# Sparse attention and two feed-forward layers in one kernel: moving the first block's feed-forward pieces among the attention units

## The chip, the cores and the metric

The kernel runs on one core of a Trainium2 chip (one of its eight NeuronCores). The metric is the device time of one execution in microseconds (us), the median over several runs. A profile of one execution comes with it; its span is the time from the first to the last profiled instruction.

## The reference

```
x = attention(q, k, v)          # 2 batches, 8 heads, 768 tokens, 64 per head; ALiBi bias, local window of 96 and 8 global keys
x = x.reshape(1536, 512)
h = x @ w_in                    # 512 x 2048
x = (h * sigmoid(h)) @ w_out    # 2048 x 512
h = x @ w_in2
out = (h * clip(h + 3, 0, 6) / 6) @ w_out2
```

The weights come as float64 and the result is float32. A float32 operand of a feed-forward product is split into a high and a low part, so that each product is three matmuls (high by high, high by low, low by high).

## The kernel before, in words

Everything is in one function. The program of each engine is written by a loop over steps n (`loop`, line 782), which emits the attention work of step n, then at most one piece of feed-forward work, then the transposes of the unit before, then late work of ScalarE (ACT) and the decoding of weights. TensorE (PE), ACT and GpSimd (POOL) run their instructions in just that order; the order on VectorE (DVE) is found by a list scheduler.

**Attention** is cut into 16 units of three steps (unit u is steps 3u to 3u+2): a batch, half of its 768 tokens and a pair of heads. A unit's chain is: transposes of q and k (`stage_a`, psA, copied out by ACT as kt at L330 and qt at L327), scores (psS, L363), bias and row minimum on DVE (L375, one instruction for each of six tiles), exponentials on ACT (L379, six instructions, two in each step), normalising on POOL (L389), transposes of the result (psT, L399, in the next unit, copied out by DVE as pt_0 and pt_2 and by ACT as pt_1), values (psO, L417, one unit later still), copied out as xh (ACT, L420) and xl (DVE, L421).

**The feed-forward** goes through the hidden dimension in eight chunks of 256 for each layer. A chunk's work on a block of tokens is two h pieces (`h_piece`, 12 matmuls, psH) and four y pieces (`y_piece`, 6 matmuls, psY). An h piece is followed by `gate_tile`: tanh on ACT (a, L505), the product on DVE (g, L512, it reads the same PSUM bank), the high part on ACT (gh, L518) and the low part on POOL (gl, L525). A y piece of the first chunk is copied out by ACT (L681). For the first chunk the blocks are 384 tokens long, and the blocks' outputs xh, xl become complete unit by unit, so most of this chunk stands among the attention units.

The list `stream` (lines 706 to 735) holds the pieces, and `when(i)` gives the step of piece i: every second step from step 17 (the last step of unit 5) on, and every step from 53 on. In the first block `None` stands for the y pieces that there are none of. In these steps all h and y pieces share one PSUM bank, the only one with the tag "f":

```
ps_bufs = {"S": 2, "o": 2, "tr": 3, "f": 1}
ring = ({"h": ("f",), "y": ("f",)}, ...)[ready[0]][kind]
```

While the units run, the weights of the next chunk are decoded beside them: da and dc on ACT (L103, L107), three instructions on DVE of which the first two are L1013 and L1019, sums on POOL, high parts on ACT (L145).

Of the kernel before, what the change touches and what calls it, by code (L numbers as in the profile page):

```python
# [28 lines left out]
def attention_ffn_kernel(ctx, tc, q, k, v, n_global, n_local, w_in1, w_out1, w_in2, w_out2, out):  # L29
    nc = tc.nc  # L30
# [9 lines left out]
    FC = 2  # L40
# [3 lines left out]
    KT = DM // P  # L44
# [17 lines left out]
    def bank(tag, name):  # L62
        return psum.tile([P, 512], F32, name=name, tag=tag, bufs=ps_bufs[tag])

    xh = xpool.tile([P, KT, NTOK], F32R, name="xh", tag="xh")
    xl = xpool.tile([P, KT, NTOK], F32R, name="xl", tag="xl")
# [88 lines left out]
    def fast(l, c):  # L155

        return c > 1
# [40 lines left out]
    PRE = 3 * NP + LAG + 1  # L198
# [3 lines left out]
    def blocks(l, c):  # L202
        return [(t, t + TB) for t in range(0, NTOK, TB)] if (l, c) == (0, 0) else BLOCKS


    beside = 3 * 6

    def when(i):
        return PRE + 2 * i if i < beside else PRE + beside + i

    slots = {}

# [253 lines left out]
    def ffn_bank(kind, name):  # L466
        ring = ({"h": ("f",), "y": ("f",)}, {"h": ("f", "S", "S"), "y": ("tr", "o", "tr", "o", "tr")}, {"h": ("S",), "y": ("f", "o", "o")})[ready[0]][kind]
        tag = ring[rot[kind] % len(ring)]
        rot[kind] += 1
        return bank(tag, name)  # L470

    def h_piece(l, c, tk, j):
        w = weights[l, c]
        ih, il = w["ih"], w["il"]
        n0, n1 = tk
        ps = ffn_bank("h", f"psH{l}_{c}_{n0}_{j}")[:, :n1 - n0]
        js = slice(j * P, (j + 1) * P)
        n = 0
        for kt in range(KT):
            for a, x in ((ih, xh), (ih, xl), (il, xh)):  # L480
                nc.tensor.matmul(ps, a[:, kt, js], x[:, kt, n0:n1], start=n == 0, stop=n == 3 * KT - 1)  # L481
                n += 1
        gate_tile(l, c, tk, j, ps)

    def gate_tile(l, c, tk, j, ps, wait=0):

        n0, n1 = tk
        if (l, c, n0) not in gs:
            if fast(l, c) and n0 == FB:
                g1 = late_pool.tile([P, 2, FC, FB], F32R, name=f"g1{l}_{c}", tag="g1")  # L490
                gs[l, c, n0] = [g1[:, 0], g1[:, 1]]
            else:
                gs[l, c, n0] = [fpool.tile([P, FC, n1 - n0], F32R, name=f"g{x}{l}_{c}_{n0}", tag=f"g{x}") for x in "hl"]
        gh, gl = gs[l, c, n0]
        t = {}
        silu = l == 0 and ready[0] > 0
        name = f"{l}_{c}_{n0}_{j}"

        def act():

            t["a"] = fpool.tile([P, n1 - n0], F32, name=f"a{name}", tag="a")
            if silu:
                nc.scalar.activation(out=t["a"], in_=ps, func=AF.Silu)
            elif l == 0:
                nc.scalar.activation(out=t["a"], in_=ps, func=AF.Tanh, scale=0.5)  # L505
            else:
                nc.scalar.activation(out=t["a"], in_=ps, func=AF.Relu, bias=three)

        def gate():
            op = dict(scalar=1.0, op0=ALU.add) if l == 0 else dict(scalar=6.0, op0=ALU.min)  # L510
            t["g"] = fpool.tile([P, n1 - n0], F32, name=f"g{name}", tag="g")
            nc.vector.scalar_tensor_tensor(out=t["g"], in0=t["a"], in1=ps, op1=ALU.mult, **op)  # L512

        def hi():
            if silu:
                nc.scalar.mul(gh[:, j, :], t["a"], 2.0)
            else:
                nc.scalar.copy(gh[:, j, :], t["g"])  # L518

        def lo():  # L520
            if silu:
                nc.vector.scalar_tensor_tensor(out=gl[:, j, :], in0=t["a"], scalar=2.0, in1=gh[:, j, :].bitcast(F32),
                                               op0=ALU.mult, op1=ALU.subtract)
            else:
                (nc.vector if ready[0] else nc.gpsimd).tensor_tensor(out=gl[:, j, :], in0=t["g"], in1=gh[:, j, :].bitcast(F32), op=ALU.subtract)  # L525

        if wait:
            late.setdefault(now[0] + wait, []).append(act)
        else:
            act()  # L530
        if not silu:
            rests.setdefault(now[0] + wait + 1, []).append(gate)
        late.setdefault(now[0] + wait + 1, []).append(hi)
        rests.setdefault(now[0] + wait + 2, []).append(lo)
# [171 lines left out]
    stream, first_piece = [], {}  # L706
    Y = lambda l, c, b: [(y_piece, l, c, BLOCKS[b], m) for m in range(KT)]
    H = lambda l, c, b: [(h_piece, l, c, BLOCKS[b], j) for j in range(FC)]
    before = []
    for l, c in chunks:  # L710
        first_piece[l, c] = len(stream)
        if fast(l, c):
            p = [(product, l, c, i) for i in (1, 6, 5, 7, 2, 4, 3)]
            y, before = before, []
            cuts = [0, 2, 3, 4, 5, 6, 7, 8] if len(y) == 8 else [0, 2, 2, 3, 3, 4, 4, 4]
            for i in range(7):
                stream += [p[i]] + y[cuts[i]:cuts[i + 1]]
            h, y = H(l, c, 2), Y(l, c, 0)
            stream += [h[0]] + y[:2] + [h[1]] + y[2:] if fast(l, c - 1) or not l else h + y
            before = Y(l, c, 1) + Y(l, c, 2)  # L720
            continue
        if (l, c) == (1, 0):

            h = H(l, c, 0) + H(l, c, 1) + H(l, c, 2)
            stream += before[:6]
            first_piece[l, c] = len(stream)
            stream += [h[0]] + before[6:] + h[1:4] + Y(l, c, 0) + h[4:5] + Y(l, c, 1)[:2] + h[5:] + Y(l, c, 1)[2:]
            before = Y(l, c, 2)
            continue
        for tk in blocks(l, c):  # L730
            hs = [(h_piece, l, c, tk, j) for j in range(FC)]
            ys, before = (before or [None] * 4)[:4], before[4:]
            stream += [hs[0], *ys[:2], hs[1], *ys[2:]]
            before += [(y_piece, l, c, tk, m) for m in range(KT)]
    stream += before

# [9 lines left out]
    for n, (i, j) in enumerate(pieces):  # L746
        ahead = aheads(i)[j]
        for off, f in decode(n):
            slots.setdefault(when(first_piece[chunks[i]]) - ahead + off, []).append(f)
        if j == 1 and fast(*chunks[i]):  # L750
            for off, f in sums(i):
                slots.setdefault(when(first_piece[chunks[i]]) - 4 + off, []).append(f)

    with tc.manual_schedule(engines=None):
# [23 lines left out]
        stage_a(0, 1)  # L778
        warm_up(1, P)
    todo = {when(i): f for i, f in enumerate(stream)}  # L780

    def loop(n):
# [280 lines left out]
```

## Time and profile before

| what | value |
|---|---|
| median of three runs | 614.27 us (613.48 to 614.62) |
| the profiled execution's own time | 613.77 us |
| its span | 611.9 us |
| PE busy | 597.8 us, 98% |
| DVE, ACT, POOL busy | 476.6, 418.2, 155.1 us |
| granted TensorE clock | 1.00 throughout |

The end of a matmul is modelled, and matmuls overlap, so PE's busy share is high even where it waits; what a piece takes is read from the start of its first matmul to the start of the next piece. The attention units end at about 120 us, and from about 127 us on PE runs feed-forward pieces without a gap.

### The profile page before, as it was taken

To read this page: it belongs to the slowest core of one execution; us is meant where nothing else is said; L and a number is where in the kernel's file an instruction comes from. 1 tells how busy PE (TensorE), PEld (TensorE's weight loads), DVE (VectorE), ACT (ScalarE), POOL (GpSimd) and SP (SyncE) were. 2 spreads that over 40 slices of the span, in tenths; PEclk is the share of its full clock that TensorE was granted. 3 is DMA by queue.
4 is the path that set the end of the run, shared out by engine and by line. 5 is a ranking of instruction groups with operands and counts; after the bars stand their busy time and mean duration, and the time that the engine had idled before them with its cause. 6 is when DMAs were issued, how large, how long until landed. Compare 5 with 4: busy or idle time off the path is not lost.

```text
span 611.9 us, 9407 instructions
## 1 busy us (share of the span) xinstructions
PE 597.8 (98%) x3144; PEld 493.9 (81%) x3144; DVE 476.6 (78%) x1049; ACT 418.2 (68%) x868; POOL 155.1 (25%) x233
## 2 busy tenths in 40 slices
PE   8899999999999999999999999999999999999996
PEld 5677788898888888888888888888888888888885
DVE  6887888886876868686766789978979797979453
ACT  5988988666666666575756767766767676757660
POOL 3777676801111111111111210011111111121200
PEclk9999999999999999999999999999999999999999
DMA  7866653205758677777777772477496868776544
GB/s 191 192 161 149 150 142 98 61 1 120 159 135 185 159 176 169 172 171 172 174 162 146 171 175 69 153 187 180 101 217 161 189 156 179 166 174 137 104 114 166
DMA packets 76426, 92.43 MB, mean 151 GB/s; under 512 B 52180, under 2 KB 52436, under 8 KB 76116
## 3 DMA queue, kind: packets, MB, share of 16 engines
q0 software_dynamic: 11520, 43.00, 37.2%
q1 hardware_dynamic: 64304, 48.54, 26.9%
q8 instruction: 27, 0.44, 0.3%
q10 hardware_dynamic: 548, 0.23, 0.1%
q14 instruction: 27, 0.22, 0.1%
HBM read 45.61 MB, written 3.15 MB: 80 GB/s over the span
## 4 chain that ended last, share of the span: by engine, by line
PE 93%; ACT 2%; DVE 2%; POOL 1%; issue 1%; DMA 0%; SPq 0%; POOLq 0%; ACTq 0%
PE psY L667 42%; PE psH L481 21%; PE psP_b L562 8%; PE psP_c L562 5%; PE psP_a L562 5%; PE psO L417 3%; PE psS_S L363 2%; PE psT L399 2%; PE psA L325 2%; PE psS_o L363 1%; PE psW L426 1%; ACT z L379 1%; DVE pt L404 1%; POOL z L389 0%; DVE z L375 0%
## 5 line engine op out<-in xcount | busy, mean ns | idle before, releaser
L696 POOL DMA_DIRECT2D y<-st x78 | 68.0, 872 | 361.6 <-ACT st L692 357.0
L692 ACT COPY st<-psY 128x512 f32<-128x512 f32 x156 | 91.2, 585 | 53.0 <-PE psY L667 49.3
L481 PE MATMUL psH<-xh,wih 128*128 128x512 f32 (+1 forms) x200 | 76.7, 383 | 0.5 <-ACT y L681 0.5
L481 PE MATMUL psH<-xl,wih 128*128 128x512 f32 (+1 forms) x200 | 76.4, 382 | 0.0
L481 PE MATMUL psH<-xh,wil 128*128 128x512 f32 (+1 forms) x200 | 76.3, 381 | 0.0
L667 PE MATMUL psY<-gh,woh 128*128 128x512 f32 (+1 forms) x152 | 58.3, 384 | 0.5 <-DVE mn L375 0.5
L667 PE MATMUL psY<-gh,wol 128*128 128x512 f32 (+1 forms) x152 | 57.5, 378 | 0.0
L667 PE MATMUL psY<-gl,woh 128*128 128x512 f32 (+1 forms) x152 | 57.4, 378 | 0.0
L667 PE MATMUL psY<-wol,gh 128*128 128x512 f32 x142 | 55.2, 389 | 0.0
L667 PE MATMUL psY<-woh,gh 128*128 128x512 f32 x142 | 55.2, 389 | 0.0
L667 PE MATMUL psY<-woh,gl 128*128 128x512 f32 x142 | 55.2, 389 | 0.0
L379 ACT ACTIVATE z<-z,mn 128x256 f32<-128x256 f32 (+1 forms) x96 | 46.3, 486 | 9.1 <-DVE mn L375 8.6
L103 ACT ACTIVATE da<-raw 128x512 f32<-128x512 f32 x64 | 43.1, 673 | 11.8 <-DMA raw<-in_moe_w_in_dram 7.7
L389 POOL TENSOR_SCALAR z<-z,sm 128x256 f32<-128x256 f32 (+1 forms) x96 | 43.5, 471 | 23.4 <-DVE sm L385 16.5
L1025 DVE SCALAR_TENSOR_TENSOR da<-raw,da 128x512 int32<-128x512 int32 x64 | 45.7, 714 | 1.0
L579 DVE TENSOR_TENSOR u<-psP_c,u 128x512 f32<-128x512 f32 x24 | 16.5, 687 | 37.7 <-ACT u L573 37.7
L481 PEld LDWEIGHTS psH<-xh,wih 128*128 128x128 f32 x200 | 37.6, 188 | 7.7 <-ACT y L681 1.2
L481 PEld LDWEIGHTS psH<-xl,wih 128*128 128x128 f32 x200 | 37.5, 188 | 7.0 <-DVE xl L591 0.4
L481 PEld LDWEIGHTS psH<-xh,wil 128*128 128x128 f32 x200 | 37.5, 188 | 6.9 <-POOL wil L148 0.4
L1013 DVE TENSOR_SCALAR da<-da 128x512 f32<-128x512 f32 x64 | 28.6, 446 | 14.3 <-ACT da L103 14.3
L129 DVE SCALAR_TENSOR_TENSOR dc<-raw,de 128x512 f32<-128x512 uint32 x56 | 38.5, 687 | 1.5 <-DVE de L1030 0.8
L134 DVE TENSOR_TENSOR dc<-dc,da 128x512 f32<-128x512 f32 x56 | 38.3, 684 | 0.4
(196 smaller groups left out, 1498.3 us busy)
## 6 DMA issues: line engine op xcount, KB each, us to landing
y<-st POOLq DMA_DIRECT2D x78, 512.0 KB, 4.9
raw<-in_moe_w_in_dram SPq DMA_DIRECT2D x32, 512.0 KB, 4.2
raw<-in_moe_w_out_dram SPq DMA_DIRECT2D x32, 512.0 KB, 3.4
rk<-in_k_dram SPq DMA_DIRECT2D x32, 96.0 KB, 3.2
rv<-in_v_dram SPq DMA_DIRECT2D x32, 96.0 KB, 2.2
rq<-in_q_dram SPq DMA_DIRECT2D x31, 96.0 KB, 3.1
out_dram<-y SPq DMA_DIRECT2D x11, 256.0 KB, 2.5
y<-yf POOLq DMA_DIRECT2D x2, 1024.0 KB, 6.6
```

The source lines that it names most:

```text
L103: nc.scalar.activation(out=t["a"], in_=raws[n][:, :, 1].bitcast(F32), func=AF.Abs)
L129: nc.vector.scalar_tensor_tensor(out=t["c"], in0=raws[n][:, :, 0].bitcast(U32), scalar=2.0 ** -52, in1=t["e"].bitcast(F32), op0=ALU.mult, ...
L134: engine.tensor_tensor(out=t["c"], in0=t["c"], in1=t["a"], op=ALU.add)
L379: nc.scalar.activation(out=z[:, t, h, :w], in_=z[:, t, h, :w], func=AF.Exp, bias=mn[:, t, h:h + 1], scale=-1.0, accum_out=sums_of[u][:, t, ...
L389: nc.gpsimd.tensor_scalar(out=z[:, t, h, :w], in0=z[:, t, h, :w], scalar1=smt[u][:, t, h:h + 1], scalar2=1.0, op0=ALU.mult, op1=ALU.mult)
L481: nc.tensor.matmul(ps, a[:, kt, js], x[:, kt, n0:n1], start=n == 0, stop=n == 3 * KT - 1)
L562: nc.tensor.matmul(ps, a[:, 2 * k + q, f * P:(f + 1) * P], x, start=p in (1, 5) and n == 0, stop=n == 5, skip_group_check=True)
L667: nc.tensor.matmul(ps[:, :rhs.shape[1]], lhs, rhs, start=n == 0, stop=n == 3 * FC - 1)
L692: nc.scalar.copy(st[:, m % 2, :], part)
L696: late.setdefault(n, []).append(lambda: nc.gpsimd.dma_start(y, st, accum_op=ALU.add))
L1013: nc.vector.tensor_scalar(out=a, in0=a, scalar1=as_float(897 << 20), scalar2=as_float((1151 << 20) - 1), op0=ALU.max, op1=ALU.min)
L1025: nc.vector.scalar_tensor_tensor(out=ai, in0=w1, scalar=-0x40000000, in1=ai, op0=ALU.bitwise_and, op1=ALU.bitwise_or)
```

## The change

The first block has two h pieces (j = 0 and 1); each is now emitted in two halves of six matmuls (the first two and the last two of the four 128-row slices of d_model), which accumulate in one bank. The four halves stand in the last steps of units 5, 6, 7 and 8 (steps 17, 20, 23, 26). The `None` entries are gone. From unit 9 on an h piece stands in the last step of every odd unit (29, 35, 41, 47, as before), and the two y pieces that follow it in the second and third step of the even unit between (31, 32, 37, 38, 43, 44, 49, 50); before, the first stood in the second step of the even unit and the second in the first step of the odd one (31, 33, 37, 39 and so on). From step 53 on the steps are the same.

```
+    STEPS = [PRE + 3 * i for i in range(4)] + [PRE + 12 + 6 * i + j for i in range(4) for j in (0, 2, 3)]
+
     def when(i):
-        return PRE + 2 * i if i < beside else PRE + beside + i
+        return STEPS[i] if i < len(STEPS) else PRE + beside + beside - len(STEPS) + i
...
-    def h_piece(l, c, tk, j):
+    begun = {}
+
+    def h_piece(l, c, tk, j, halves="ab"):
...
-        ps = ffn_bank("h", f"psH{l}_{c}_{n0}_{j}")[:, :n1 - n0]
+        if "a" in halves:
+            begun[0] = ffn_bank("h", f"psH{l}_{c}_{n0}_{j}")[:, :n1 - n0]
+        ps = begun[0]
...
+            if "ab"[kt * 2 // KT] in halves:
...
+        if "b" in halves:
+            gate_tile(l, c, tk, j, ps)
...
-            hs = [(h_piece, l, c, tk, j) for j in range(FC)]
-            ys, before = (before or [None] * 4)[:4], before[4:]
-            stream += [hs[0], *ys[:2], hs[1], *ys[2:]]
+            halves = ("a", "b") if not stream else ("ab",)
+            hs = [[(h_piece, l, c, tk, j, half) for half in halves] for j in range(FC)]
+            ys, before = before[:4], before[4:]
+            stream += [*hs[0], *ys[:2], *hs[1], *ys[2:]]
```

What this does to the engines' programs, at three places. The lines of the changed kernel are numbered two higher from line 208 on, six higher in `gate_tile` and `y_piece`, seven higher in the decoding functions.

**PE and ACT, units 10 and 11.** Before, PE's first y piece (psY_0_0_0, y of block 0, rows 0 to 127 of the output) is followed by the transposes psT; the words in brackets are the engines it has to wait for:

```order
L325 MATMUL psA_1_1308<-ident,rq_1084 128x128 x2
L667 MATMUL psY_0_0_0_1319<-gh_0_0_749,woh_885 128x384 [waits DVE_49]
L667 MATMUL psY_0_0_0_1319<-gl_0_0_750,woh_885 128x384
L667 MATMUL psY_0_0_0_1319<-gh_0_0_749,wol_886 128x384 [waits Pool_49]
L399 MATMUL psT_0_1337<-ident,z_1131 128x128 [waits DVE_49,Pool_49]
```

and in the change the second y piece stands between them and waits for ACT:

```order
L327 MATMUL psA_1_1308<-ident,rq_1072 128x128 x2
L673 MATMUL psY_0_0_0_1319<-gh_0_0_856,woh_881 128x384 [waits DVE_49]
L673 MATMUL psY_0_0_0_1319<-gl_0_0_857,woh_881 128x384 [waits Pool_49]
L673 MATMUL psY_0_0_0_1319<-gh_0_0_856,wol_882 128x384
L673 MATMUL psY_0_0_1_1337<-gh_0_0_856,woh_881 128x384 [waits Activation_49]
L401 MATMUL psT_0_1345<-ident,z_1127 128x128 [waits DVE_49]
```

ACT's program there, before (z are exponentials):

```order
L327 ACTIVATE qt_1284<-psA_1_1308,small 128x384
L681 COPY y_0_1326<-psY_0_0_0_1319 128x384
L379 ACTIVATE z_1254,eps_89<-z_1254,mn_1255 128x256 x2
L402 COPY pt_1_1347<-psT_1_1342 128x512
L103 ACTIVATE da_1357<-raw_702 128x512
L379 ACTIVATE z_1369,eps_90<-z_1369,mn_1370 128x128 x2
L420 CAST xh<-psO_1376 128x384
L330 COPY kt_1396<-psA_0_1398 128x3x128
L681 COPY y_0_1326<-psY_0_0_1_1404 128x384
```

and in the change:

```order
L329 ACTIVATE qt_1284<-psA_1_1308,small 128x384
L687 COPY y_0_1326<-psY_0_0_0_1319 128x384
L381 ACTIVATE z_1254,eps_89<-z_1254,mn_1255 128x256 x2
L687 COPY y_0_1326<-psY_0_0_1_1337 128x384
L404 COPY pt_1_1355<-psT_1_1350 128x512
L103 ACTIVATE da_1365<-raw_702 128x512
L381 ACTIVATE z_1377,eps_90<-z_1377,mn_1378 128x128 x2
```

The copy of the second y piece moved from the odd unit to the even one, ahead of pt_1. The same pattern stands in units 12, 13 and 14, 15.

**DVE, at the start of unit 13.** Before, the first score tile of unit 13 (z_1613) comes ahead of the decoding of the next weights (da):

```order
L404 COPY pt_2_1596<-psT_2_1591 128x512
L384 TENSOR_REDUCE sm_1501<-eps_89 128x2
L375 ISA z_1613,mn_1614<-psS_S_1601,distA 128x256
L375 ISA mn_1614 128x1
L385 RECIPROCAL sm_1501<-sm_1501 128x2
L375 ISA z_1613,mn_1614<-psS_S_1602,distA 128x256
L1013 TENSOR_SCALAR da_1599<-da_1599 128x512
```

and in the change two instructions of the decoding stand ahead of the first score tile:

```order
L406 COPY pt_0_1590<-psT_0_1587 128x2x128
L406 COPY pt_2_1604<-psT_2_1599 128x512
L1020 TENSOR_SCALAR da_1607<-da_1607 128x512
L1026 TENSOR_SCALAR da_1607<-da_1607 128x512
L377 ISA z_1621,mn_1622<-psS_S_1609,distA 128x256
```

The scheduler put L1020 and L1026 (L1013 and L1019 before) in front of unit 13's scores; at unit 15 it is the same, at unit 11 only the first of them.

**PE, units 5 and 6.** Before, unit 5 has a whole h piece ahead of its transposes, and unit 6 none; in the change each has half of one. Unit 5 in the change:

```order
L327 MATMUL psA_1_715<-ident,rq_514 128x128 x2
L487 MATMUL psH_0_0_0_736<-xh,wih_444 128x384
L487 MATMUL psH_0_0_0_736<-xl,wih_444 128x384
L487 MATMUL psH_0_0_0_736<-xh,wil_445 128x384
L401 MATMUL psT_0_743<-ident,z_561 128x128 [waits Activation_49,Pool_49]
L401 MATMUL psT_1_750<-ident,z_561 128x128 [waits DVE_49,Pool_49]
L401 MATMUL psT_2_757<-ident,z_561 128x128 [waits Activation_49,Pool_49]
```

The three kinds of psH rows come twice. The last group, psT_2, waits for ACT's qt in units 5 to 8 (in units 6 and 8 before it waited for DVE alone).

## Rows read from the trace of the kernel before

**Rows 1.** The page, part 1: busy us, share, instructions of each engine.

```profile
PE 597.8 (98%) x3144; PEld 493.9 (81%) x3144; DVE 476.6 (78%) x1049; ACT 418.2 (68%) x868; POOL 155.1 (25%) x233
```

**Rows 2.** Windows: busy us (instructions) of PE, PEld, DVE, ACT, POOL; clock; DMA.

```profile
37.35:71.22 33.87, 31.94 (x312) 26.73 (x309) 27.53 (x112) 29.38 (x91) 26.10 (x45) 1.00 0.68 164
71.22:99.76 28.54, 27.72 (x252) 23.67 (x250) 24.04 (x92) 25.38 (x78) 20.35 (x34) 1.00 0.56 138
```

**Rows 3.** Timeline of PE, units 12 and 13: start, duration, group, [idle before <-releaser].

```profile
86.78 0.42 PE L667 MATMUL psY<-gh,woh 128*128 128x384 f32 x1
...
87.92 0.82 PE L399 MATMUL psT<-ident,z 128*128 128x128 f32 x6
...
92.53 0.42 PE L667 MATMUL psY<-gh,woh 128*128 128x384 f32 x1
...
94.40 0.45 PE L481 MATMUL psH<-xh,wih 128*128 128x384 f32 x1 [0.24 <-ACT y L681]
```

**Rows 4.** Timeline of ACT, units 12 to 14.

```profile
85.30 0.51 ACT L379 ACTIVATE z<-z,mn 128x256 f32<-128x256 f32 x1 [0.97 <-DVE mn L375]
...
88.99 0.47 ACT L681 COPY y<-psY 128x384 f32<-128x384 f32 x1
...
90.34 0.57 ACT L402 COPY pt<-psT 128x512 f32<-128x512 f32 x1
90.81 0.71 ACT L103 ACTIVATE da<-raw 128x512 f32<-128x512 f32 x1
91.39 0.53 ACT L379 ACTIVATE z<-z,mn 128x256 f32<-128x256 f32 x1
...
93.87 0.48 ACT L681 COPY y<-psY 128x384 f32<-128x384 f32 x1 [0.57 <-PE psY L667]
...
99.76 0.51 ACT L379 ACTIVATE z<-z,mn 128x256 f32<-128x256 f32 x1 [1.04 <-DVE mn L375]
```

**Rows 5.** Timeline of DVE, units 12 and 13.

```profile
84.84 0.42 DVE L375 CUSTOM_DVE_ANT_0 z<-psS_S,distA 128x256 f32<-128x256 f32 x1
...
91.55 0.76 DVE L1013 TENSOR_SCALAR da<-da 128x512 f32<-128x512 f32 x1
```

**Rows 6.** The page, part 5: the same line over the whole span, busy, mean ns.

```profile
L1013 DVE TENSOR_SCALAR da<-da 128x512 f32<-128x512 f32 x64 | 28.6, 446 | 14.3 <-ACT da L103 14.3
```

**Rows 7.** Timeline of ACT, units 10 and 11.

```profile
71.22 0.40 ACT L379 ACTIVATE z<-z,mn 128x128 f32<-128x128 f32 x1 [1.17 <-DVE mn L375]
...
74.69 0.47 ACT L681 COPY y<-psY 128x384 f32<-128x384 f32 x1
...
77.10 0.39 ACT L379 ACTIVATE z<-z,mn 128x128 f32<-128x128 f32 x1
```

**Rows 8.** Timeline of PE, units 5 and 6.

```profile
42.45 0.50 PE L363 MATMUL psS_S<-kept,qt 64*128 64x128 f32 x4
...
48.15 0.63 PE L399 MATMUL psT<-ident,z 128*128 128x128 f32 x4 [0.44 <-DVE pt L404]
```

**Rows 9.** Timeline of ACT, units 5 and 6.

```profile
37.35 0.51 ACT L379 ACTIVATE z<-z,mn 128x256 f32<-128x256 f32 x1
...
40.08 0.57 ACT L327 ACTIVATE qt<-psA,small 128x384 f32<-128x384 f32 x1
...
44.21 0.51 ACT L379 ACTIVATE z<-z,mn 128x256 f32<-128x256 f32 x1 [1.45 <-DVE mn L375]
```

**Rows 10.** Timeline of ACT, units 14 and 15.

```profile
103.82 0.53 ACT L681 COPY y<-psY 128x128 f32<-128x128 f32 x2
...
106.37 0.51 ACT L379 ACTIVATE z<-z,mn 128x256 f32<-128x256 f32 x1
```

**Rows 11.** Timeline of PE, from unit 15 to the last block's h piece.

```profile
109.44 0.45 PE L667 MATMUL psY<-gh,woh 128*128 128x384 f32 x1 [0.53 <-DVE mn L375]
...
121.47 0.44 PE L481 MATMUL psH<-xh,wih 128*128 128x384 f32 x1
```

**Rows 12.** Timeline of PE, unit 1: transposes after a long wait.

```profile
15.95 1.06 PE L399 MATMUL psT<-ident,z 128*128 128x128 f32 x8 [0.90 <-DVE kt L335]
```

More of the change, by code (lines that the diff above doesn't have):

```diff
@@ L475, in h_piece @@
         n0, n1 = tk
-        ps = ffn_bank("h", f"psH{l}_{c}_{n0}_{j}")[:, :n1 - n0]
+        if "a" in halves:
+            begun[0] = ffn_bank("h", f"psH{l}_{c}_{n0}_{j}")[:, :n1 - n0]
+        ps = begun[0]
         js = slice(j * P, (j + 1) * P)
-        n = 0
         for kt in range(KT):
[L480 to L483, printed above, removed]
+            if "ab"[kt * 2 // KT] in halves:
+                for a, x in ((ih, xh), (ih, xl), (il, xh)):
+                    nc.tensor.matmul(ps, a[:, kt, js], x[:, kt, n0:n1], start=kt == 0 and x is xh and a is ih, stop=kt == KT - 1 and a is il)
+        if "b" in halves:
+            gate_tile(l, c, tk, j, ps)
     def gate_tile(l, c, tk, j, ps, wait=0):
```

## The prediction

> **What bounds the kernel now.** I read the page first. PE is busy 98% of the span [rows 1], and from about 127 us on the pieces follow each other without a gap, so whatever the change wins or loses among the attention units passes to the end unshortened, and nothing behind them is moved. The windows come next: among the units PE is nearly full, but so is ACT, 29.38 of 33.87 us from unit 5 to unit 10 and 25.38 of 28.54 us from there to unit 14 [rows 2]; the granted clock is 1.00 in both. Then the timelines, engine by engine. The reader should see in them a cycle that is closed by ACT: a unit's first exponentials wait for DVE's minimum of the scores (idle 0.97 to 1.45 us before them [rows 4, 7, 9]), and the rest of ACT's unit runs without a pause. I therefore measure a unit from its first exponentials to the next one's: units 10 and 11 take 85.30 - 71.22 = 14.08 us [rows 4, 7], units 12 and 13 take 99.76 - 85.30 = 14.46 us [rows 4].
>
> **The halves, units 5 to 8.** No matmul is added. A half is six of an h piece's twelve, as many as a y piece has, which takes 1.14 us with its launch (86.78 to 87.92 [rows 3]). Unit 5 loses six; its third group of transposes (four, 0.12 us each) now waits for qt, which ends at 40.08 + 0.57 = 40.65 [rows 9], so unit 6's scores start at about 41.2 in place of 42.45 [rows 8]. ACT idled 1.45 us before unit 6's first exponentials [rows 9], so that they can follow: about 1.2 us won. Unit 6 takes six matmuls; what was a transposing group at 48.15 [rows 8] now waits for qt of unit 7 as well, and its ACT work was already without a pause; I give back 0.3. Unit 7 loses six like unit 5, but behind a unit that is late already: half of what unit 5 gave, 0.6 won. Units 8 and 9 take a half and a gh (0.5 us of ACT) from a neighbour that loses it: nothing. Sum -1.5 us. The bounds: 0, if ACT's idle time only moves, and -4.5, if all of it (33.87 - 29.38 [rows 2]) went; I stay near the first, because qt now stands ahead of the transposes in all four units.
>
> **The y pieces, units 10 to 15.** This is the larger term. Both pieces of an even unit write the one bank "f", and on PE nothing stands between them any more, so the second waits for ACT's copy of the first. ACT does that copy behind the second pair of exponentials and qt: in unit 12 the piece starts at 86.78 and PE is through with it at 87.92 [rows 3], but the copy runs from 88.99 to 89.46 [rows 4]. Before, PE used these 1.5 us for the transposes of the unit before. Now they queue behind the second piece, and behind them the next unit's scores.
>
> One pair worked out, units 12 and 13, counted from unit 12's first exponentials at 85.30. The first copy ends at +4.16, as before, since nothing new stands ahead of it. The second piece runs from +4.2 to +5.3 (1.14 us, 86.78 to 87.92 [rows 3]). Ten transposes of 0.12 us (eight took 1.06 with the end of the last [rows 12]) bring PE to +6.5, pt_1 can start at about +6.2 and ends at +6.8 (0.57), da at +7.4 (0.71 less the usual overlap) [rows 4]; before, da was done at 91.52, +6.2. DVE now has the clamp and the shift of da ahead of unit 13's scores. The clamp took 0.76 us at this place, beside POOL's work [rows 5], and 0.446 in the mean of the page [rows 6]; I take 0.76 for it, which is the nearer row, and 0.5 for the shift, which will run partly beside POOL. That is +8.7, and from the start of a score tile to the first exponential it takes 85.30 - 84.84 = 0.46 us [rows 4, 5]: +9.1, where it was 91.39 - 85.30 = 6.09 [rows 4].
>
> Unit 13 gains: from its first exponentials to those of unit 14 it took 99.76 - 91.39 = 8.37 us; the copy of 0.48 and the wait of 0.57 for it [rows 4] leave it, and with them the 0.24 for which PE's h piece idled for this copy [rows 3], which lay beside them. 8.37 - 1.05 = 7.3. The pair: 9.1 + 7.3 = 16.4 against 14.46, +2.0 us. With the mean of 0.446 for both DVE instructions it is +1.6, with 0.8 for both +2.3.
>
> Units 10 and 11 in the same way: copy done at 74.69 + 0.47 - 71.22 = +3.9 [rows 7], the second piece to +5.1, pt_1 to +6.6, da to +7.2, only the clamp ahead of the scores (0.76), then 0.3 for a tile of half the width: +8.3 where it was 77.10 - 71.22 = 5.88 [rows 7]. Unit 11 took 8.20, now 7.15 by the same two terms. 15.45 against 14.08, +1.4 us.
>
> Units 14 and 15: the copies end at 103.82 + 0.53 = 104.35 [rows 10], 4.6 after 99.76; the second piece to +5.75, its own copies to +6.5, pt_1 to +7.4, da to +8.0, clamp and shift to +9.3, first exponentials of unit 15 at +9.7 where they were 106.37 - 99.76 = 6.6 [rows 4, 10], +3.1. Behind unit 15 a piece of 1.14 us is gone, and so is the hole in which PE idled 0.53 us in front of the next one [rows 11]; some of the transposes' waits go with it. I leave +1.0 at the last block's first h piece, which started at 121.47 [rows 11].
>
> Edits at no cost: moving gl on POOL and two loads on the SP queue by a place or two. POOL is the least busy of the four compute engines, 20.35 of 28.54 us [rows 2], and ACT's idle time at the exponentials is put down to DVE and at the copies to PE [rows 4, 7, 9], none of it to a load; if a load came late, da would, and the scores behind it. The copies write the same y tile in the same sequence and no DMA of the first chunk hangs on them.
>
> **Sum.** -1.5 + 1.4 + 2.0 + 1.0 = +2.9 us. The profiled execution took 613.77 us itself (span 611.9), which gives 616.7. The median of the runs is 614.27, 0.5 higher, which I leave in the range. 0.2% of it, 1.2 us, is about the least that a measurement of this kernel can tell from no change: slower begins at 615.5, faster at 613.0.
>
> **The rivals.** (1) Faster: the second piece does not wait. Then the halves' 1.5 us stay, and in each of three pairs the h piece's idle 0.24 us [rows 3] goes, 0.7 us: 611.6. That holds if ACT copies the first piece before PE is through with it, 1.5 us earlier than at 88.99. Nothing in ACT's order allows that while qt and the exponentials stand ahead. Chance 0.07.
>
> (2) No change: PE stalls, but the odd unit catches up, so that each even unit's first exponentials come 1.9 us after its scores as before, and DVE's da does not hold up the scores. Then only PE's chain counts: per pair the stall of 1.54 us (87.92 to 89.46), less the 0.24 in front of the h piece [rows 3] and a wait among the transposes like the 0.44 of [rows 8], +0.86 in two pairs, and less the 0.53 of [rows 11] also in the last, +0.3. With -1.5 it is +0.5, 614.3. For it: the odd unit sheds 1.05 us of ACT time; against: ACT has little idle time left in which to catch up [rows 2]. Chance 0.17.
>
> (3) Slower by more: nothing is won in units 5 to 8, because their transposes now all wait for qt, and DVE's da takes 0.8 us twice beside POOL. 0 + 1.7 + 2.3 + 1.1 = +5.1 gives 618.9. Chance 0.15.
>
> (4) The clock falls. PE would idle some 1.5 to 2.5 us three times. The longest wait among the units here was 0.90 us; the eight transposes after it took 1.06 us, the full pace, and the granted clock stayed 1.00 [rows 2, 12]. A fall to half, the lower of its two levels, for the transposes, scores and values behind each stall (3.9 us each) would add up to 11.7 us: 628. Chance 0.03. The Trainium skill (TensorE: Matmul & The Clock Gate, section "A second HAM failure mode: psum-queue depth-cycling") tells of a kernel that cycles through PSUM, idles briefly between groups of matmuls and swings between 1.2 and 2.4 GHz. By that rule this change would set it off and the time would be that of this rival; by the row the clock term is nothing, and no run here yet shows a longer wait among matmuls.
>
> **How the numbers follow.** The forecast has what is left, 0.58, and is the likeliest: 616.7. Its own terms spread from 614.8 (-2.5 for the halves, and 1.1 + 1.6 + 0.8 with the low DVE prices) to 618.3 (-0.5, and 1.7 + 2.3 + 1.0). The range 613.4 to 619.1 takes in the second and third rival and leaves out the first, the fourth and the edges. Slower: of the forecast 0.50, and the third and fourth rival, 0.68. Within 0.2%: the rest of the forecast and most of the second rival, 0.23. Faster: the first rival and an edge of the second, 0.09.
>
> **What would show it.** PE waits for ACT's y copy (L687) between two y pieces in units 10, 12 and 14, over 1.5 us each; the time from first exponentials to first exponentials of units 12 and 13 together is near 16.4 us, and from unit 5's to unit 10's near 32.4 us (33.87 before). The clock stays 1.00. I am wrong if the second y piece follows the first without a wait, if the pairs take 14 us as before, if units 5 to 9 take as long as before or shed over 3 us, or if the difference lies behind the attention units.

## The result and the profile after

| | before | after |
|---|---|---|
| median of six executions each | 614.34 us (613.48 to 614.94) | 617.98 us (615.65 to 619.92) |
| ratio | | 1.0057 [1.0043, 1.0071] |
| the profiled execution's own time, span | 613.77, 611.9 us | 615.65, 613.7 us |

Slower, by 3.6 us in the medians and by 1.9 us between the two profiled executions. A second series (experiment 4) gave 617.05 against 614.65 us, 1.0047 [1.0029, 1.0065]. The traces account for the 1.9 (1.8 between the spans); what makes most other executions of the changed kernel longer is not shown by a trace, and the last section tells what points to a place ahead of unit 5.

The page of the changed kernel has a smaller busy share of PE (97% against 98% in [rows 1], with the same 3144 matmuls) and a new wait in the entry for the y pieces (busy, mean ns, idle before and what ended it):

```profile
PE 596.5 (97%) x3144; PEld 492.9 (80%) x3144; DVE 473.4 (77%) x1049; ACT 417.8 (68%) x868; POOL 154.7 (25%) x233
...
L673 PE MATMUL psY<-gh,woh 128*128 128x512 f32 (+1 forms) x152 | 58.2, 383 | 4.9 <-ACT y L687 4.9
```

In the page of before the same entry has:

```profile
L667 PE MATMUL psY<-gh,woh 128*128 128x512 f32 (+1 forms) x152 | 58.3, 384 | 0.5 <-DVE mn L375 0.5
```

PE waits 4.9 us for ACT's y copies, in three places. The timeline of PE shows them, each at the first matmul of an even unit's second y piece (units 10, 12, 14); the line at 98.25 is unit 14's scores, the last two are the last block's first and second h piece:

```profile
70.45 0.43 PE L673 MATMUL psY<-gh,woh 128*128 128x384 f32 x1
...
73.17 0.44 PE L673 MATMUL psY<-gh,woh 128*128 128x384 f32 x1 [1.42 <-ACT y L687]
...
85.61 0.43 PE L673 MATMUL psY<-gh,woh 128*128 128x384 f32 x1
...
88.56 0.44 PE L673 MATMUL psY<-gh,woh 128*128 128x384 f32 x1 [1.66 <-ACT y L687]
...
89.72 1.25 PE L401 MATMUL psT<-ident,z 128*128 128x128 f32 x10
...
98.25 0.50 PE L365 MATMUL psS_S<-kept,qt 64*128 64x128 f32 x4
...
104.92 0.44 PE L673 MATMUL psY<-gh,woh 128*128 128x384 f32 x1 [1.77 <-ACT y L687]
...
123.02 0.44 PE L487 MATMUL psH<-xh,wih 128*128 128x384 f32 x1
...
126.25 0.33 PE L487 MATMUL psH<-xh,wih 128*128 128x384 f32 x1
```

In the trace of before the second h piece starts here:

```profile
124.53 0.33 PE L481 MATMUL psH<-xh,wih 128*128 128x384 f32 x1
```

The timeline of ACT gives the first exponentials of units 5, 10, 11, 12, 13 and 14, between those of 12 and 13 the two copies, pt_1 and da, and at the end unit 14's copies of its first y piece:

```profile
37.00 0.51 ACT L381 ACTIVATE z<-z,mn 128x256 f32<-128x256 f32 x1
...
68.78 0.40 ACT L381 ACTIVATE z<-z,mn 128x128 f32<-128x128 f32 x1 [0.37 <-DVE mn L377]
...
77.24 0.40 ACT L381 ACTIVATE z<-z,mn 128x128 f32<-128x128 f32 x1 [0.83 <-DVE mn L377]
...
84.45 0.51 ACT L381 ACTIVATE z<-z,mn 128x256 f32<-128x256 f32 x1 [0.97 <-DVE mn L377]
...
88.05 0.47 ACT L687 COPY y<-psY 128x384 f32<-128x384 f32 x1
...
89.92 0.48 ACT L687 COPY y<-psY 128x384 f32<-128x384 f32 x1 [0.41 <-PE psY L673]
...
90.63 0.58 ACT L404 COPY pt<-psT 128x512 f32<-128x512 f32 x1 [0.23 <-PE psT L401]
91.11 0.69 ACT L103 ACTIVATE da<-raw 128x512 f32<-128x512 f32 x1
93.57 0.51 ACT L381 ACTIVATE z<-z,mn 128x256 f32<-128x256 f32 x1 [1.77 <-DVE mn L377]
...
100.74 0.51 ACT L381 ACTIVATE z<-z,mn 128x256 f32<-128x256 f32 x1 [0.97 <-DVE mn L377]
...
104.34 0.53 ACT L687 COPY y<-psY 128x128 f32<-128x128 f32 x2
```

And on DVE clamp and shift stand ahead of unit 13's first score tile:

```profile
91.91 0.67 DVE L1020 TENSOR_SCALAR da<-da 128x512 f32<-128x512 f32 x1 [0.20 <-ACT da L103]
92.61 0.59 DVE L1026 TENSOR_SCALAR da<-da 128x512 int32<-128x512 int32 x1
93.12 0.41 DVE L377 CUSTOM_DVE_ANT_0 z<-psS_S,distA 128x256 f32<-128x256 f32 x1
```

With the same marks in every trace the time splits into four stages: from unit 5's first exponentials to unit 10's, to unit 12's, to unit 14's, and to the last block's second h piece. That last mark has the same work ahead of it in all fourteen traces, 1002 matmuls on PE. The first h piece, which the prediction names, has not: 985 in before, 984 in the change and 981 in experiments 3, 5, 7, 8, 11 and 12, since some y matmuls of 0.17 us stand ahead of it in one kernel and behind it in another. All numbers in us; each is the difference of two such starts.

| kernel | 5 to 10 | 10 to 12 | 12 to 14 | 14 to second h piece | sum | of 12 to 14: unit 12 |
|---|---|---|---|---|---|---|
| before | 33.87 | 14.08 | 14.46 | 24.77 | 87.18 | 6.09 |
| after | 31.78 | 15.67 | 16.29 | 25.51 | 89.25 | 9.12 |
| 1 halves alone | 31.78 | 14.49 | 14.46 | 24.77 | 85.50 | 6.08 |
| 2 pairs alone | 33.86 | 15.28 | 16.31 | 25.50 | 90.95 | 9.14 |
| 3 two banks | 31.78 | 14.44 | 16.15 | 25.21 | 87.58 | 7.14 |
| 4 the change again | 31.79 | 15.68 | 16.30 | 25.49 | 89.26 | 9.14 |
| 5 piece behind transposes | 31.80 | 14.56 | 16.01 | 24.82 | 87.19 | 8.61 |
| 6 da later | 31.78 | 15.78 | 15.67 | 26.20 | 89.43 | 8.23 |
| 7 two banks, da later | 31.80 | 14.43 | 14.45 | 23.64 | 84.32 | 6.78 |
| 8 halves everywhere | 31.56 | 15.43 | 16.40 | 27.17 | 90.56 | 7.02 |
| 9 halves, da later | 31.79 | 14.59 | 14.47 | 24.54 | 85.39 | 5.80 |
| 10 before, da later | 33.91 | 14.21 | 14.46 | 24.54 | 87.12 | 5.78 |
| 11 as 7, again | 31.80 | 14.45 | 14.45 | 23.68 | 84.38 | 6.76 |
| 12 behind, da later | 31.80 | 14.67 | 14.60 | 24.03 | 85.10 | 7.13 |

Stages of one program repeat within 0.04 us (the change and 4, 7 and 11), whatever the execution's own time, so this table is sharper than the medians.

### The profile page after: what moved, and what is told of

Read it like the earlier page. It is cut to its first block, busy times and chain, and to the rows that moved or that the text cites. A ratio compares the mean times of both kernels' runs of the same rounds, so it can differ in the third digit from the quotient of the medians.

```text
span 613.7 us, 9411 instructions
## 1 busy us (share of the span) xinstructions
PE 596.5 (97%) x3144; PEld 492.9 (80%) x3144; DVE 473.4 (77%) x1049; ACT 417.8 (68%) x868; POOL 154.7 (25%) x233
## 4 chain that ended last, share of the span: by engine, by line
PE 89%; ACT 5%; DVE 3%; issue 1%; POOL 1%; ACTq 0%; DVEq 0%; POOLq 0%
PE psY L673 42%; PE psH L487 20%; PE psP_b L568 8%; PE psP_c L568 5%; PE psP_a L568 5%; PE psT L401 2%; ACT z L381 2%; PE psO L419 2%; PE psS_S L365 2%; DVE z L377 1%; PE psA L327 1%; PE psS_o L365 1%; ACT qt L329 1%; ACT kt L332 1%; ACT xh L422 0%
## 5 line engine op out<-in xcount | busy, mean ns | idle before, releaser
L1032 DVE SCALAR_TENSOR_TENSOR da<-raw,da 128x512 int32<-128x512 int32 x64 | 44.1, 690 | 1.1
L1020 DVE TENSOR_SCALAR da<-da 128x512 f32<-128x512 f32 x64 | 28.4, 444 | 14.3 <-ACT da L103 14.0
```

Source lines behind the costliest of these rows:

```text
L1020: nc.vector.tensor_scalar(out=a, in0=a, scalar1=as_float(897 << 20), scalar2=as_float((1151 << 20) - 1), op0=ALU.max, op1=ALU.min)
L1032: nc.vector.scalar_tensor_tensor(out=ai, in0=w1, scalar=-0x40000000, in1=ai, op0=ALU.bitwise_and, op1=ALU.bitwise_or)
```

## The experiments

Experiments 1 to 4 ran on one chip (before: 614.65 us, 23 executions), 5 to 8 on a second (614.51, 19), 9 to 11 on a third (614.89, 24) and 12 on a last one (615.33, 11).

**1. The halves alone.** In the changed kernel:

```
-    STEPS = [PRE + 3 * i for i in range(4)] + [PRE + 12 + 6 * i + j for i in range(4) for j in (0, 2, 3)]
+    STEPS = [PRE + 3 * i for i in range(4)] + [PRE + 12 + 2 * i for i in range(12)]
```

> Only the halves of the first block's h pieces in units 5 to 8; the y pieces stand where they stood before the change. Theory (the change is the sum of two parts that touch only by their order): from unit 5's first exponentials to unit 10's 31.8 us as in the changed kernel (33.87 before), nothing lost later, so about 612.4 us, 1.9 under the kernel before, clock 1.00 in every execution. Rival (units 10 and on give it back, because ACT and DVE set the pace there): 613.8 to 614.5, with the time from unit 10's first exponentials to unit 14's over 29.5 us (28.54 before).

613.62 us, ratio 0.998 [0.9967, 0.9994]. The first stage is that of the change to 0.01 us, and units 10 and 11 lose 0.4. The halves are a gain of 1.7 us that the change gives away. The median lies 1.2 us above what was expected, the fastest execution (612.06) 0.3 below it. The clock was expected at 1.00 in every execution; in nine of twelve its mean is 0.994 to 0.999.

**2. The pairs alone.**

```
-    STEPS = [PRE + 3 * i for i in range(4)] + [PRE + 12 + 6 * i + j for i in range(4) for j in (0, 2, 3)]
+    STEPS = [PRE, PRE + 6] + [PRE + 12 + 6 * i + j for i in range(4) for j in (0, 2, 3)]
...
-            halves = ("a", "b") if not stream else ("ab",)
+            halves = ("ab",)
```

> Only the pairs: whole h pieces at units 5 and 7 as before the change, both y pieces of an even unit in a row as in the change. Theory of the PSUM bank alone: +1.6 (units 10, 11) +1.8 (units 12, 13) +0.6 (units 14, 15) as in the changed kernel's profile, 618.3 us, clock 1.00. Rival (TensorE's clock falls behind the waits in most executions, and that is the rest of the changed kernel's +3.6): 619.5 to 621, with a mean granted clock of 0.995 to 0.998 in most executions and a stretch under 1.00 within a few us of a wait for the y copy.

618.62 us, 1.0069 [1.0056, 1.0082], near the 618.3 of the theory of the bank. The first stage is that of before, the other three lose 1.20 + 1.85 + 0.73 = 3.78 us. The two parts of the change add up: -1.68 and +3.77 make +2.09, the change has +2.07. In this trace PE waits 1.43, 1.69 and 1.78 us for the y copies, and the clock stands at 1.00 from 20 to 600 us: the rival, a clock that falls behind the waits, is not borne out.

**3. A second bank.** The second y piece of a pair writes a bank of the ring of three, so that it waits for no copy:

```
-        ring = ({"h": ("f",), "y": ("f",)}, ...
+        ring = ({"h": ("f",), "y": ("f", "tr")}, ...
```

> The change, but the second y piece of a pair takes a bank of the ring of three (tr) in place of the one bank f. Theory (the wait for ACT's copy is the whole loss of the pairs): no wait between the two y pieces, 612.2 to 613.2 us, clock 1.00 in every execution. Rival 1 (two pieces in a row hold up the transposes, da and the scores anyway, by the 1.1 us of a piece in each pair): units 12 and 13 near 15.5 us, 614.5 to 615.5. Rival 2 (the bank is missing to the transposes): a new wait of over 0.5 us ahead of psT or psA, 615 to 618.

614.90 us, 0.9997 [0.9983, 1.0011]. The time lies where the first rival put it, but not for its reason. The wait is gone in all three places, but in units 12 and 13 only 0.14 of 1.83 us comes back, against the theory; unit 13 now takes 9.01 us (7.17 in the change). The timelines of PE, DVE and POOL in unit 13:

```profile
88.25 0.35 PE L673 MATMUL psY<-gh,wol 128*128 128x384 f32 x1
88.43 0.34 PE L673 MATMUL psY<-gh,woh 128*128 128x384 f32 x1
...
98.18 0.44 PE L487 MATMUL psH<-xl,wih 128*128 128x384 f32 x1 [1.77 <-DVE xl L423]
```

```profile
92.67 1.35 DVE L1020 TENSOR_SCALAR da<-da 128x512 f32<-128x512 f32 x1
...
94.98 1.39 DVE L1026 TENSOR_SCALAR da<-da 128x512 int32<-128x512 int32 x1
```

```profile
92.47 1.27 POOL L126 TENSOR_TENSOR dc<-dc,de 128x512 f32<-128x512 f32 x1
...
94.79 1.29 POOL L134 TENSOR_TENSOR dc<-dc,da 128x512 f32<-128x512 f32 x1
```

The second piece follows the first in 0.18 us. But clamp and shift now fall between unit 13's minima, each 0.2 us behind the start of one of POOL's two operations on dc (decoding of weights, like da), and each ends 0.28 us behind that operation, at 94.02 and 96.37 (92.47 + 1.27 = 93.74, 94.79 + 1.29 = 96.08). They take 1.35 and 1.39 us in place of 0.67 and 0.59, xl is late by that, and PE's h piece waits 1.77 us for xl: a new wait of the size of the old one.

**4. The change again.**

> The changed kernel once more, to see its executions one by one: with clock 1.00 all through, 615.5 to 616 us; with a mean clock of 0.995 to 0.997, 617.5 to 620. If the clock falls because of the waits, a trace with a mean under 1.00 shows the low stretch within a few us behind a wait for the y copy; if the fall has another cause (the start, the end), it lies elsewhere and the kernel before has it too.

617.05 us, 1.0047 [1.0029, 1.0065]. Four of its and the first series' twelve executions take 615.65 to 616.17 us, the other eight 617.55 to 619.92. In the two traces to be had the clock stands at 1.00 from 20 us to the end of the units; where it fell in the longer executions no trace shows; what the traces of 3 and 10 have is told in the last section.

**5. The second piece behind the transposes**, in the one bank f:

```
         f = todo.get(n)
-        if f:
+        second = n in STEPS and n - 1 in STEPS
+        if f and not second:
             f[0](*f[1:])
         turns(n)
+        if f and second:
+            f[0](*f[1:])
```

> The change, but the second y piece of a pair is issued behind the transposes of its step, ahead of the next unit's scores; bank f stays its only bank. Theory (what costs is that transposes, pt_1 and da queue behind the waiting piece): the copy of the first piece is done when the transposes are, the wait for it falls under 0.5 us; the odd unit's first exponentials come 1.1 us later than in the kernel before (7.2 us after the even unit's, 6.09 before), and the odd unit sheds 1.05; units 12 and 13 near 14.5 us (16.29 in the changed kernel), the halves' 2.1 us stay: ratio to the kernel before 0.996 to 0.998. Rival (any pair of pieces in one unit costs, wherever it stands): units 12 and 13 over 15.5 us, ratio 1.000 or more.

614.45 us, 0.9999 [0.9988, 1.0011]. No wait for a copy is listed any more, the order alone does that. Units 12 and 13 stay at 16.01 us, as the rival has it, but not for its reason: here too the clamp lies beside POOL's operation on dc, ahead of unit 13's minima, and the h piece waits for xl:

```profile
91.26 1.48 DVE L1023 TENSOR_SCALAR da<-da 128x512 f32<-128x512 f32 x1 [1.21 <-ACT da L103]
```

```profile
96.89 0.45 PE L487 MATMUL psH<-xl,wih 128*128 128x384 f32 x1 [1.52 <-DVE xl L423]
```

**6. da one step later**, with what follows it in the decoding:

```
-            return ((PRE, 11, 5, -1), (33, 27, 21, 15))[i]
+            return ((PRE, 11, 5, -1), (33, 26, 20, 14))[i]
```

> The change, with the decoding of three weight pieces (da and what follows) one step later, so that da stands at the start of units 11, 13 and 15 in place of the end of the unit before; the loads behind it move along. Theory (of the pairs' loss, DVE's clamp and shift ahead of the odd unit's scores are 1.2 us in units 12 and 13, and less in the others): the wait for the y copy stays at 1.66 us, unit 13's first exponentials come 7.9 us after unit 12's (9.12 in the changed kernel), ratio 1.000 to 1.002. Rival (the two instructions then run beside POOL's products, at 1.35 us each as in the kernel with two banks, and hold up unit 13's minima or xl): units 12 and 13 still over 16 us, ratio 1.003 to 1.006.

618.01 us, 1.0052 [1.0036, 1.0068]: nothing is won, and the time that the theory gave is missed. Unit 13's first exponentials do come sooner, 8.23 us after unit 12's in place of 9.12, and clamp and shift take 0.43 us each, behind all minima. But with the wait for the copy still there (1.56 us in unit 12) unit 13 gives 0.27 of it back, units 10 and 11 lose 0.11 and the last stage 0.69. In that stage PE waits for POOL's gl, here first, then in the changed kernel:

```profile
120.88 0.44 PE L673 MATMUL psY<-gl,woh 128*128 128x384 f32 x1 [1.30 <-POOL gl L531]
```

```profile
118.59 0.44 PE L673 MATMUL psY<-gl,woh 128*128 128x384 f32 x1 [0.64 <-POOL gl L531]
```

This wait is longer by 0.66 us; what delays gl there was not taken apart.

**7 and 11. Both: two banks and da later.** The edits of 3 and 6.

> Both: the second y piece in the ring of three banks, and da one step later. Theory (the wait and DVE's da are the whole loss, and the kernel with two banks kept only the second): units 12 and 13 near 14.7 us (16.15 with two banks alone), ratio 0.996 to 0.998. Rival (DVE's da costs the same wherever it stands beside POOL): over 15.8 us, ratio 0.999 to 1.001 as with two banks alone.

611.63 us, 0.9955 [0.9940, 0.9970], and once more:

> The kernel with two banks and a later da once more, beside the two others of this group on the same chip. If its gain holds, the ratio is again 0.994 to 0.997; if it lay with that chip, 0.998 or more.

612.12 us, 0.9959 [0.9943, 0.9975]. Units 12 and 13 are back at 14.45, and the last stage falls to 23.64, 1.13 us under that of before. Alone, the second bank took 1.67 us off the change's sum and the later da added 0.18; together they take 4.93. ACT's first exponentials of units 12, 13 and 14, and DVE's pair in unit 13:

```profile
85.21 0.51 ACT L381 ACTIVATE z<-z,mn 128x256 f32<-128x256 f32 x1 [0.50 <-DVE mn L377]
...
91.99 0.51 ACT L381 ACTIVATE z<-z,mn 128x256 f32<-128x256 f32 x1 [0.86 <-DVE mn L377]
...
99.66 0.51 ACT L381 ACTIVATE z<-z,mn 128x256 f32<-128x256 f32 x1 [0.66 <-DVE mn L377]
```

```profile
94.66 1.00 DVE L1020 TENSOR_SCALAR da<-da 128x512 f32<-128x512 f32 x1 [0.38 <-ACT da L103]
95.69 0.43 DVE L1026 TENSOR_SCALAR da<-da 128x512 int32<-128x512 int32 x1
```

**8. Halves in all blocks.** h halves in the last step of every unit from 5 to 16, a y piece in the second step of every unit from 10 on, in the ring of three banks:

```
+    STEPS = sorted([PRE + 3 * i for i in range(12)] + [PRE + 14 + 3 * i for i in range(7)] + [51])
...
+            halves = ("a", "b") if (l, c) == (0, 0) else ("ab",)
...
+            stream += [x for pair in zip(hs[0] + hs[1], ys) for x in pair] if ys and len(halves) == 2 else [*hs[0], *ys[:2], *hs[1], *ys[2:]]
...
+        ring = ({"h": ("f",), "y": ("tr",)}, ...
```

> No pairs: the h pieces of all three blocks of the first chunk in halves, one in the last step of each unit from five to sixteen, and one y piece in the second step of each unit from ten on, in the ring of three banks, since a half-filled f is in use. Theory (what the halves won in units 5 to 8 is that each unit carries the same six matmuls, and this goes on): the 2.1 us of units 5 to 9 and another 1 to 2 us up to unit 14, ratio 0.994 to 0.996. Rival (from unit 10 ACT and DVE set the pace, and each unit now has a y copy between its second exponentials and the transposes): no further gain, ratio 0.997 to 0.999, or a loss with the odd units' da, up to 1.002.

617.78 us, 1.0054 [1.0039, 1.0069], worse than every number that was expected. The first stage gains another 0.2 us, all later ones lose against before. What the loss is made of was not taken apart; its longest pause is 2.46 us on ACT ahead of unit 14's first exponentials, beside the third da instruction of DVE, which takes 1.64 us.

**9 and 10. da later without pairs**, to see whether that edit wins by itself: the halves alone, and the kernel before, each with the edit of 6.

> The halves alone (y pieces where they stood before the change), with da one step later. It tells whether the gain of the kernel with two banks and a later da comes from da alone or from the pairs. Theory (da alone: without a wait the place of the y pieces matters little): 14.5 us for units 12 and 13, about 20 us from unit 14's first exponentials to the last block's h piece as there (21.71 before), ratio 0.994 to 0.997. Rival (the pairs give the end its gain, since nothing is left for unit 15 and behind): as with the halves alone, over 21.4 us there, ratio 0.997 to 1.000.

> The kernel before, with da one step later and nothing else. Theory (in the kernel before, DVE's clamp and shift fall behind the first minima of the odd units already, so that a later da gives them nothing): ratio 0.999 to 1.001. Rival (da has a price of its own in every odd unit, whatever stands around it): ratio 0.995 to 0.998.

612.58 us, 0.9967 [0.9953, 0.9981], and 615.60 us, 1.0003 [0.9988, 1.0019]. In the kernel before a later da is worth 0.06 us of the stages, on the halves 0.11, and 9 takes 21.48 us to the first h piece, the mark of its expectation, as the rival had it. So of the 1.18 us that 7 wins over 1 in the stages, 1.07 come with the pairs and their second bank, 0.90 of them in the last stage (23.64 against 24.54 in 9). The executions alone do not show it: 612.12 in 11 and 612.58 in 9, with intervals that overlap.

**12. Behind the transposes, da later.** The edits of 5 and 6, with the one bank f.

> The second y piece behind the transposes in the one bank f, as in the earlier run, with da one step later. Theory (what is left in units 12 and 13 once the wait is gone is DVE's clamp and shift, which POOL's work on dc holds up, whatever took the wait away): units 12 and 13 near 14.5 us (16.01 with the piece behind the transposes alone), ratio 0.995 to 0.997, as with two banks and a later da. Rival (the second bank itself gave that gain): units 12 and 13 over 15.5 us, ratio 0.999 to 1.002.

611.89 us, 0.9947 [0.9927, 0.9966]. Units 12 and 13 take 14.60. It is the second way to take the wait away, and with it, too, the rest of the loss goes with da. 7 and 12 beat both kernels; between them the stages favour 7 (84.32 and 85.10), and the ratios overlap.

## Why the prediction was right

The forecast was 616.7 us and slower; the profiled execution took 615.65, the median 617.98, both inside the range. The mechanism is the forecast one: PE waits for the first piece's copy, and transposes, pt_1, da and the next scores come late by it. That 616.7 lies between the two times is in part luck: the traces' +1.9 is less than the forecast +2.9, and the further 1.8 us of the medians come from something that the forecast does not contain. Point by point:

- **The halves**, forecast -1.5. Measured -2.09 in the first stage (33.87 to 31.78), the same in experiment 1. Unit by unit, from first exponentials to first exponentials: unit 5 gave -1.12 (forecast -1.2), unit 6 +0.02 (+0.3), unit 7 -0.43 (-0.6), together -1.53 as forecast. What was mis-sized are units 8 and 9, put at nothing: -0.04 and -0.52. Of the latter 0.41 is that unit 10's first exponentials come 1.49 us behind its scores in place of 1.90; unit 10 in its turn takes 0.41 longer with the halves alone, so that they win -1.68 over all stages. The transposes do wait for qt, 0.42 us in unit 6.
- **Units 10 and 11**, forecast +1.4, measured +1.59, of which 0.4 are also there with the halves alone; the pairs alone (experiment 2) cost 1.20.
- **Units 12 and 13**, forecast +2.0, as 9.1 + 7.3. Measured 9.12 + 7.17, +1.83. Each step of that chain stands in the rows of the result, counted from 84.45: copy done at +4.07 (forecast +4.16), pt_1 at +6.18 (+6.2), da done at +7.35 (+7.4), the first score tile behind clamp and shift at +8.67 (+8.7). The clamp took 0.67 (0.76), the shift 0.59 (0.5). The working starts from a unit's first exponentials waiting for DVE; in before that holds for the even units, while those of units 11 and 13 stand right behind da, without a pause [rows 4, 7].
- **Units 14, 15 and the end**, forecast +1.0 at the last block's first h piece, measured +0.56 there (21.71 to 22.28) and +0.74 at the second. The wait in unit 14 is the longest, 1.77 us. The forecast took the end of the copies from before, +4.6; they end at +4.13 (104.34 + 0.53 - 100.74), and unit 15's first exponentials come at +9.17 in place of +9.7, 2.56 later than before and not 3.1. The saving behind unit 15 came out as forecast, 2.0 of 2.1 us to the first h piece.
- **The sum**, forecast +2.9, measured +2.07 in the stages. The two terms that were mis-sized are units 8 and 9 (0.56 us, of which 0.41 went back in unit 10) and unit 14 (0.5 us).
- **The signs.** The waits were to be over 1.5 us each: the one in unit 10 is 1.42. Units 12 and 13 took 16.29 (near 16.4), unit 5 to 10 31.78 (near 32.4).
- **The rivals.** The first (no wait) fell, 1.42 to 1.77 us were waited. The second (the odd unit catches up) fell too: unit 13 gave back 1.20 us (8.37 to 7.17) of the 3.03 that unit 12 lost (6.09 to 9.12), with DVE's da ahead of unit 13's minima; the third (nothing won by the halves) fell with the first stage. The fourth fell as it was put: behind waits of 1.42, 1.66 and 1.77 us among the matmuls the granted clock stayed 1.00, its upper level of 2.4 GHz, in the trace of the changed kernel, and in those of experiments 2 and 4. So the rule of the Trainium skill (TensorE: Matmul & The Clock Gate, section "A second HAM failure mode: psum-queue depth-cycling") did not apply to these waits.

What the forecast did not see is how its two causes hang together. It added the wait for the copy and DVE's da as steps of one chain, so taking away either should have won its share. Experiments 3, 5 and 6 say otherwise for units 12 and 13: of their 1.83 us the two edits that take the wait away win 0.14 and 0.28 (in units 10 and 11 they do win, 15.67 to 14.44 and 14.56). Without the wait clamp and shift slide to where POOL's operations on dc hold them, and a wait for xl takes the place of the wait for y; with the wait, moving them wins 0.62 us in units 12 and 13, which is lost again elsewhere. Only 7 and 12, which remove both, show that pairs are no loss in themselves: in place of +4.16 (15.67 + 16.29 + 25.51 less 14.08 + 14.46 + 24.77) the three stages make -0.79 in experiment 7 and -0.01 in 12.

## What to carry to other kernels

Before two pieces that share one PSUM bank are put in a row, look at where the copy of the first stands in its engine's own order: the second waits for all that is ahead of it there, and everything behind the second waits along. When a wait is removed and the time does not move, look for the work that it had sheltered (here DVE's clamp and shift, which beside the wait met only the last part of POOL's instructions, 0.67 and 0.59 us, and without it nearly the whole of them, 1.35 and 1.39), and try both edits together. A table of stage times from the same marks in every trace separates parts of a change at 0.1 us, where single executions scatter by 2 or more. Count the work ahead of a mark before comparing it: ahead of the last block's first h piece it differs by up to four matmuls, 0.7 us, which is more than some of the gains in question.

## What the runs showed of the hardware that was not expected

**DVE's clamp and shift are held until POOL's instruction ends.** In the fourteen traces there are 112 of these two instructions (128x512, in place) between 60 and 121 us. Started while POOL was at nothing (31 of them), they took 0.41 to 0.43 us. 81 started while an instruction of POOL was running. Of these 69 were prolonged, and each ended 0.28 to 0.29 us after that instruction, whether it was an operation on dc, a product with sm or gl; the longest took 1.48 us. The other 12 started in the instruction's last 0.16 us. The price depends on when in POOL's instruction they start, and so the forecast's choice between 0.446, 0.76 and 0.8 was a choice among accidents. The Trainium skill (SBUF — State Buffer, section "Who interferes with whom") says that a VectorE operation of this kind, when it runs in a mode that uses two ports, and one of GpSimd take a shared pair of ports in turn, and that the second to issue is blocked for the whole of the first. These rows agree; the mode itself no trace shows.

**Half the clock after a pause at 20 us, ahead of all that was changed.** At about 20 us PE's next transposes of rq come after a pause: 0.40 us in the profiled execution of before, 1.21 in that of after, 2.70 in that of experiment 3. That they wait for the load of rq is inferred: this load has no landing in the traces, but the SP queue issues it at 17.46 us in experiment 3 and at 16.00 in before, and the next loads of rq land at 23.70 and 21.79. The windows around it (busy by engine, then granted clock, DMA share, GB/s):

```profile
22.31 0.87 PE L327 MATMUL psA<-ident,rq 128*128 128x128 f32 x3 [2.70 <-issue]
```

```profile
16.00:20.00 4.00, 3.62 (x41) 2.66 (x39) 3.54 (x19) 3.57 (x13) 3.47 (x7) 1.00 0.78 190
20.00:22.00 2.00, 0.00 (x0) 0.00 (x0) 0.90 (x3) 1.73 (x6) 1.76 (x3) 0.90 1.15 264
22.00:25.00 3.00, 2.69 (x13) 2.50 (x13) 1.35 (x4) 1.72 (x5) 0.32 (x1) 0.50 0.56 123
25.00:30.00 5.00, 4.40 (x46) 3.24 (x44) 3.98 (x21) 4.06 (x13) 3.86 (x7) 1.00 0.81 207
```

PE does nothing for 2.70 us and then works at 0.50, its lower level of 1.2 GHz, for 3 us; unit 5's first exponentials come 2.4 us later than in the changed kernel (39.43 against 37.00). The order of before has it too: in the trace of experiment 10 the same wait is 2.73 us, and the clock 0.61 from 22 to 25 us:

```profile
21.93 0.52 PE L325 MATMUL psA<-ident,rq 128*128 128x128 f32 x3 [2.73 <-issue]
```

This is where executions of one kernel differ by 2 us and more, on instructions that stand in the same order in both kernels. Experiments 7 and 11 are one program: there the pause is 2.01 and 1.11 us, the clock from 22 to 26 us 0.59 and 1.00, and unit 5's first exponentials come at 38.98 and 36.86. It may be what lifts most of the eight longer executions of the changed kernel above 617.5 us: five of them have mean clocks of 0.995 and 0.996, as the traces of 3 and 10. But this is not shown. There is no trace of any of the eight, two have 0.997, which the trace of 11 has without the pause (its clock is 1.00 from 20 to 600 us and falls only at the end), one (618.20 us) has 1.00, and why there are more of them than in the kernel before stays open; it may be chance, since 28 of the 77 executions of the kernel before beside experiments 1 to 12 have 0.997 or less.
